# TensorE work of the last stage in column tiles of 128 rows by 32 columns

## The chip, the cores and the metric

The kernel runs on one core of one Trainium2 chip. Time is device microseconds (us) of that core; the number used is the median of the runs shown. TensorE is the matrix engine (PE in the profile, its weight loads PEld), VectorE is DVE, ScalarE is ACT, GpSimd is POOL, SyncE is SP. All DMAs of this kernel are issued by SP.

## The reference

Inputs are bfloat16, with S = 2048 rows and D = 512 columns; F is 1376. The forward pass is

```python
xn = layernorm(A_q)
k_shift = causal 4-tap filter of k with shift_k;  kv = k_shift * v
y = causal convolution of kv with ssm_k, + kv * ssm_D        # by FFT of length 2S
out = A_q + xn * y + ((xn @ w_gate) * (xn @ w_up)) @ w_down
```

What must be returned is `out` and the gradients, for a given `grad_out`, with respect to A_q, A_k, A_v, shift_k, ssm_k, ssm_D and the three weights. The kernel computes the FFTs as products with tables of sines and cosines.

## The kernel before

**Stages.** (1) Layer norm, and for six slices of F the products g, u and dh and their gradients h, dg, du, which go to DRAM (`HD`) or stay in SBUF. (2) The weight gradients (`dw_gen`). (3) The first step of the transforms (`a_gen`, through `AX`), then the middle step (`s_gen`), whose result goes to `CX` in DRAM. (4) The last stage, lines 888 to 950, from about 278 us (its first transforms still among the last weight gradients) to the end. It works in eight chunks n, each of two groups of 128 rows.

**The last stage.** For chunk n:
- `c_load(n)` (line 650) loads 1.5 MB of `CX` into one buffer `f["C"]`. There is one such buffer, so the load of chunk n+1 waits until TensorE has read chunk n.
- `last_dft(n)` (lines 694 to 702) makes the last transform step: 12 products of 64 output rows by 512 columns. Halves h = 0 and 1 go to PSUM partitions 0 to 63 and 64 to 127, so two run side by side in the array. ScalarE copies the three results out (`c_dkv`, `c_y`, `c_o5`), and VectorE multiplies and adds them.
- `c_dsk(n)` (line 739, the gradient of shift_k) sums over the rows what VectorE has multiplied, with a weight of 32 columns of ones: 8 products of 32 output rows, in four column tiles (PSUM partitions 0, 32, 64 and 96).
- `y_o(n, rr)` (line 759) is out: 11 products of 128 by 512 accumulated in one PSUM half bank of 128 by 512, read by VectorE at once, or in the last chunk by ScalarE after one more product with the identity.
- `y_x(n, rr)` (line 776) is the gradient of xn: 22 such products, then six VectorE operations and one of ScalarE, which end in the gradient of A_q.
- `dk_pair` is the gradient of k: seven VectorE operations on 128 by 1024.

The left operands of `y_o` and `y_x` (`hd_block`) are h, dg and du with F on the partitions. Those that went to DRAM are read back by a transposing DMA (`hd_load(n)`, line 616, two buffers). Those that stayed in SBUF are transposed by TensorE in `turn_gen` (line 593): batches of eight 128 by 128 transposes into one PSUM tile, copied out by ScalarE. The batches of slice NST - 1 number 12, the first with k = 0.

**What sets the order.** Every engine call goes through class `Eng` (line 143), which only records it. Consecutive TensorE calls on the same PSUM slots become one `Op`. `emit` (line 181) then emits the `Op`s in an order that is written out in `PLAN`, a packed constant, with the PSUM place of each. The scheduler of the framework is off: each engine runs its instructions in that order. Because all calls are made in `Eng.call`, nearly every line in the profile is L173.

A product with a left operand of 128 rows by c columns occupies c columns of TensorE's array. In the last stage of the kernel before, three widths alternate: 128 (`y_o`, `y_x`, transposes), 64 (`last_dft`) and 32 (`c_dsk`).

Of the kernel before, what the change touches and what calls it, by code (L numbers as in the profile page):

```python
# [18 lines left out]
D = 512  # L19
F = 1376  # L20
R = 16
NFB = 11
NST = 6
# [4 lines left out]
NCH = 8  # L28
# [9 lines left out]
def kernel(  # L38
# [24 lines left out]
    nc = tc.nc  # L63
# [17 lines left out]
    def v3(ap, a):  # L81
        return ap.rearrange("p (a b) -> p a b", a=a)

    def bfv(ap, a, b):
        return ap.bitcast(BF)[:, 0:a * b].rearrange("p (a b) -> p a b", a=a)
# [29 lines left out]
    def rF(kind="F"):  # L115
        slots.append(Slot(2, kind))
        return PV(slots[-1], lambda b: b)

    def rN(kind="G"):
        slots.append(Slot(1, kind))  # L120
        return PV(slots[-1], lambda b: b)
# [12 lines left out]
    def together():  # L134
        hold[0] = []

    def apart():
        hold[0] = None

    def fix(x):  # L140
        return x.at(x.slot.base) if isinstance(x, PV) else x

    class Eng:


        def __init__(self, name, real):
            self.name = name; self.real = real

        def __getattr__(self, meth):
            f = getattr(self.real, meth)  # L150

            def call(*a, **k):
                last = ops[-1] if ops else None
                own = []
                for x in list(a) + list(k.values()):
                    if isinstance(x, PV) and x.slot not in own:
                        own.append(x.slot)
                cols = k["rhs"].shape[-1] if meth == "matmul" and not isinstance(k["rhs"], PV) else 128
                if meth == "matmul":
                    cols = 1  # L160
                    for n in k["rhs"].shape[1:]:
                        cols *= n
                if self.name == "PE" and hold[0]:
                    o = hold[0][0]
                elif (self.name == "PE" and hold[0] is None and last is not None and last.eng == "PE" and last.slots == own
                      and last.cols + cols <= 2200 and last.prio == now[0]):
                    o = last
                else:
                    o = Op(self.name, now[0])
                    ops.append(o)  # L170
                    if self.name == "PE" and hold[0] is not None:
                        hold[0].append(o)
                o.fns.append(lambda: f(*[fix(x) for x in a], **{kk: fix(x) for kk, x in k.items()}))  # L173
                o.uses.append((meth, a, k))
                o.cols += cols
                for s in own:
                    if s not in o.slots:
                        o.slots.append(s)
            return call
# [20 lines left out]
    nc = NC  # L200
# [5 lines left out]
    MM = nc.tensor.matmul  # L206
# [4 lines left out]
    def place(shape, dt, at):  # L211
        n = 1
        for s in shape[1:]:
            n *= s
        if dt == BF:
            v = big[0:shape[0], at // 2:at // 2 + n]
        else:
            v = big[0:shape[0], at // 2:at // 2 + 2 * n].bitcast(dt)
        if len(shape) == 3:
            return v.rearrange("p (a b) -> p a b", a=shape[1])  # L220
        if len(shape) == 4:
            return v.rearrange("p (a b c) -> p a b c", a=shape[1], b=shape[2])
        return v
# [23 lines left out]
    ident = rc.tile("ident", [128, 128])  # L247
    W12 = rc.tile("W12", [128, 192])
    W1 = W12[:, 0:128]
    W2 = W12[:, 128:192]  # L250
# [22 lines left out]
    def slot(j, r):  # L273
        return RH + 1536 * ((RO[j] + r) % RING)

    def ring(j, r, n=1):
        if j != 1:
            return place([128, n, 768], BF, slot(j, r)).rearrange("p r (t f) -> p r t f", t=3)
        return place([128, n, 384], BF, slot(1, 0) + 768 * r).rearrange("p r (t f) -> p r t f", t=3)[:, :, :, 32:128]
# [146 lines left out]
    def hd_at(b, odd):  # L426
        return 640 + 128 * b if odd else 128 * ((b + 1) % 4)
# [138 lines left out]
    f = {}  # L566
# [26 lines left out]
    def turn_gen():  # L593
        for j, r0 in ((NST - 2, R - KEEP), (NST - 1, 0)):
            blk = [(r, t, b) for r in range(r0, R) for t in range(3) for b in (0, 128)]
            for k in range(0, len(blk), 8):
                pt = bfv(rN(), 8, 128)
                for i, (r, t, b) in enumerate(blk[k:k + 8]):
                    nc.tensor.transpose(pt[:, i, :], ring(j, r)[:, 0, t, b:b + 128], ident[:])
                r, b = blk[k][0], k % 6  # L600
                ACOPY(place([128, 8, 128], BF, slot(j, r) + 256 * b), pt)
                yield

    wy = {n: place([128, NFB, D], BF, 76 * KB + 11264 * i) for i, n in enumerate("dgu")}
# [8 lines left out]
    def hd_span(n):  # L613
        return (0, 1152) if 2 * n < R - KEEP else (128, 1024)
# [5 lines left out]
    def hd_block(m, t, fb):  # L620
        h = hdP[m // 2 % 2]
        a = hd_span(m // 2)[0]
        if fb == 10:
            return h[:, 3 * (m % 2) + t, 512 - a:640 - a]
        if fb >= 8 or fb >= 6 and m >= R - KEEP:
            return place([128, 6, 128], BF, slot(fb // 2 + 1, m))[:, 2 * t + fb % 2, :]
        c = hd_at(fb // 2, m % 2) - a
        return h[:, 2 * t + fb % 2, c:c + 128]
# [65 lines left out]
    def last_dft(n):  # L694
        py = f["py"] = [v3(rF(), 2) for sig in range(3)]
        C = f["C"]
        together()
        for sig in (1, 0, 2):
            for rr in range(2):
                for h in range(2):  # L700
                    MM(py[sig][64 * h:64 * h + 64, rr, :], lhsT=W2, rhs=C[:, 2 * h + rr, sig * D:sig * D + D], start=True, stop=True)
        apart()

    def c_y(n):
# [54 lines left out]
    def y_o(n, rr):  # L759
        m = f["m"][n % 2]  # L760
        end = n == NCH - 1
        for c in (slice(0, 256), slice(256, 512)) if end and rr == 1 else (slice(0, 512),):
            po = rN("y")
            for fb in range(NFB):
                MM(po[:, c], lhsT=hd_block(2 * n + rr, 0, fb), rhs=wy["d"][:, fb, c], start=(fb == 0), stop=(fb == NFB - 1 and not end))
            if end:
                MM(po[:, c], lhsT=ident[:], rhs=m[:, rr, c], start=False, stop=True)
                ACOPY(m[:, rr, c], po[:, c])
            else:
                TT(m[:, rr, c], m[:, rr, c], po[:, c], op=ALU.add)  # L770
        if end:
            st(o0[:, 2 * n + rr, :], m[:, rr, :])
        elif rr == 1:
            st(o0[:, 2 * n:2 * n + 2, :], m[:])

    def y_x(n, rr):
        r = 2 * n + rr
        rs = slice(2 * n, 2 * n + 2)
        px = rN("y")
        for t, w in ((1, "g"), (2, "u")):  # L780
            for fb in range(NFB):
                MM(px, lhsT=hd_block(2 * n + rr, t, fb), rhs=wy[w][:, fb, :], start=(t == 1 and fb == 0), stop=(t == 2 and fb == NFB - 1 and n + 1 < NCH))
        e = t = f["e"][n % 2]; dxn = f["dxn"]
        if n + 1 == NCH:
            MM(px, lhsT=ident[:], rhs=e[:, rr, :], start=False, stop=True)
            nc.scalar.activation(dxn[:, rr, :], px, ACTF.Identity, accum_out=s1[:, r:r + 1])
        else:
            STT(dxn[:, rr, :], e[:, rr, :], 1.0, px, op0=ALU.mult, op1=ALU.add, accum_out=s1[:, r:r + 1])
        STT(e[:, rr, :], dxn[:, rr, :], 1.0, xn[:, r, :], op0=ALU.mult, op1=ALU.mult, accum_out=s2[:, r:r + 1])
        r1 = slice(r, r + 1)  # L790
        TS(c2[:, r1], s2[:, r1], -1.0 / D, None, op0=ALU.mult)
        STT(c1[:, r1], s1[:, r1], -1.0 / D, rstd[:, r1], op0=ALU.mult, op1=ALU.mult)
        STT(dxn[:, rr, :], xn[:, r, :], c2[:, r1], dxn[:, rr, :], op0=ALU.mult, op1=ALU.add)
        nc.scalar.activation(t[:, rr, :], dxn[:, rr, :], ACTF.Identity, bias=c1[:, r1], scale=rstd[:, r1])
        TT(t[:, rr, :], t[:, rr, :], go[:, r, :], op=ALU.add)
        if rr == 1:
            st(o1[:, rs, :], t[:])
# [94 lines left out]
    for _ in turn_gen():  # L892
        pass
# [16 lines left out]
    for n in range(NCH):  # L910
        last = n + 1 == NCH
        t = F0 + n * DF
# [3 lines left out]
        if n >= 1 and not last:  # L916
            dk_pair(2 * n - 2)
        at(t)
        y_o(n, 0)
        if not last:  # L920
            at(t + DF * .15)
            c_y(n + 1)
        at(t + DF * .2)
        y_x(n, 0)
        if not last:
            at(O0 + OJ * (n + 1))
# [124 lines left out]
```

## Time and profile before

| | us |
|---|---|
| median of 3 runs (lowest to highest) | 432.94 (431.38 to 433.23) |
| span of the profiled execution | 429.5 |
| the median over that span | 3.4 |
| TensorE busy in the span | 419.6 |
| VectorE busy | 352.8 |
| ScalarE busy | 267.3 |
| granted TensorE clock, mean | 1.000 |

The profile holds one execution. The span runs from the first to the last instruction; launch and completion lie around it, and no time of the profiled execution as a whole is recorded, so the spread of the three runs stands for it. Times in the views are us from the span's start. In the timeline view a row is: start, duration, engine, line, operation, output <- input with the shape, xcount, and in brackets the idle time ahead of it and what ended it. "128\*64" is the part of the array that the weight occupies, rows by columns. TensorE's busy time counts overlapped matmuls and is not a measure of its peak; start-to-start times are used instead.

### The profile page before, as it was taken

What the parts mean: (1) busy time and instruction counts of PE and PEld (TensorE: products, weight loads), DVE (VectorE), ACT (ScalarE), POOL (GpSimd) and SP (SyncE); (2) the same over time, 40 slices, a digit from 0 to 9 for tenths busy, and PEclk for the clock granted to TensorE, in tenths of its full rate; (3) what the DMA queues carried; (4) which work ended last, traced back from release to release, by engine and by line L of the source; (5) the groups of instructions that cost most, each with busy time, mean ns of one, the idle gap of its engine ahead of it and who ended that gap; (6) DMA issues with size and microseconds to landing.
All of it is one profiled execution on the core that took longest, in us unless ns stands there. A gap on an engine that the chain in (4) does not pass through costs nothing.

```text
span 429.5 us, 8151 instructions
## 1 busy us (share of the span) xinstructions
PE 419.6 (98%) x3174; PEld 204.1 (48%) x3174; DVE 352.8 (82%) x684; ACT 267.3 (62%) x374; POOL 3.5 (1%) x9
## 2 busy tenths in 40 slices
PE   7999999999999999999999999889999999999996
PEld 4665455754454333544444344444444544444443
DVE  6799979998549989899999981044869989999996
ACT  2986879698554998988989963664244340313323
POOL 1000000000000000000000000000000000000000
PEclk9999999999999999999999999999999999999999
DMA  7997787959796979989989989999999999999933
GB/s 249 401 405 240 281 305 264 370 214 381 295 338 200 322 274 306 316 254 338 321 250 315 340 282 254 241 363 336 265 290 267 310 256 317 306 282 301 284 150 124
DMA packets 94878, 124.65 MB, mean 290 GB/s; under 512 B 53748, under 2 KB 63865, under 8 KB 93816
## 3 DMA queue, kind: packets, MB, share of 16 engines
q1 hardware_dynamic: 94840, 124.13, 91.7%
q8 instruction: 25, 0.41, 0.4%
q14 instruction: 13, 0.11, 0.1%
HBM read 57.10 MB, written 54.04 MB: 259 GB/s over the span
## 4 chain that ended last, share of the span: by engine, by line
PE 91%; DMA 6%; DVE 1%; SPq 1%; issue 1%; ACT 0%; ACTq 0%
PE PP L173 91%; DMA big<-CX 4%; DMA big<-in_goT_dram 1%; DVE big L173 1%; SPq L173 1%; ACT big L173 0%; ACTq L173 0%
## 5 line engine op out<-in xcount | busy, mean ns | idle before, releaser
L173 PE MATMUL PP<-big 128*128 128x512 bf16 (+9 forms) x3174 | 419.6, 347 | 5.8 <-issue 1.8
L173 PEld LDWEIGHTS <-big 128*128 128x128 bf16 (+5 forms) x3174 | 204.1, 98 | 221.0 <-issue 65.2
L173 DVE TENSOR_TENSOR big<-big 128x1024 bf16<-128x1024 bf16 (+4 forms) x465 | 269.3, 629 | 46.0 <-ACT big L173 42.6
L173 ACT CAST big<-PP 128x512 bf16<-128x512 f32 (+2 forms) x314 | 225.2, 780 | 90.0 <-PE PP L173 74.8
L173 ACT ACTIVATE big<-big 128x512 bf16<-128x512 f32 (+3 forms) x30 | 19.1, 645 | 40.8 <-DVE big L173 40.8
L173 DVE CAST big<-PP 128x512 bf16<-128x512 f32 (+1 forms) x37 | 32.3, 873 | 11.9 <-PE PP L173 10.0
L173 ACT COPY big<-PP 128x1024 bf16<-128x1024 bf16 x25 | 24.9, 1019 | 21.5 <-PE PP L173 21.5
L173 DVE SCALAR_TENSOR_TENSOR big<-big 128x1 f32<-128x1 f32 (+2 forms) x52 | 25.5, 498 | 0.6 <-ACT big L173 0.2
L173 DVE BATCH_NORM_STATS2 big<-big 128x6 f32<-128x512 bf16 x16 | 10.8, 679 | 2.7 <-DMA big<-in_x_dram 2.6
L173 DVE TENSOR_TENSOR big<-big,PP 128x512 bf16<-128x512 bf16 x14 | 9.5, 682 | 4.1 <-PE PP L173 4.0
L173 DVE SCALAR_TENSOR_TENSOR big<-big,PP 128x512 f32<-128x512 bf16 x14 | 9.5, 682 | 3.3 <-PE PP L173 3.3
L173 DVE TENSOR_SCALAR big<-big 128x1 f32<-128x1 f32 (+1 forms) x28 | 7.0, 259 | 0.2
L173 POOL MEMSET big<- 128x1536 bf16 (+2 forms) x3 | 2.8, 950 | 256.0 <-PE PP L173 252.7
L173 ACT ACTIVATE big<-PP 128x512 f32<-128x512 f32 x2 | 1.2, 598 | 5.5 <-PE PP L173 5.5
L173 DVE RECIPROCAL big<-big 128x2 f32<-128x2 f32 (+1 forms) x9 | 1.4, 155 | 3.7 <-ACT big L173 3.7
L173 DVE BATCH_NORM_AGGREGATE big<-big 128x2 f32<-128x6 f32 x16 | 2.8, 177 | 0.2
L173 ACT ACT_TABLE_LOAD x1 | 1.3, 1283 | 0.7 <-PEq L1039 0.7
L173 DVE DVE_READ_ACCUMULATOR big<-big 128x1 f32 x16 | 1.3, 81 | 0.0
L173 DVE DVE_READ_ACCUMULATOR big<-big,PP 128x1 f32 x14 | 1.1, 81 | 0.0
L173 DVE MEMSET big<- 128x1 f32 (+1 forms) x2 | 0.2, 112 | 0.8 <-PEq L1039 0.8
L173 DVE COPY big<-PP 128x1024 bf16<-128x1024 bf16 x1 | 0.7, 685 | 0.0
L173 ACT ACTIVATION_READ_ACCUMULATOR big<-PP 128x1 f32 x2 | 0.4, 194 | 0.0
(6 smaller groups left out, 0.9 us busy)
## 6 DMA issues: line engine op xcount, KB each, us to landing
HD<-big SPq DMA_DIRECT2D x32, 384.0 KB, 8.2
AX<-big SPq DMA_DIRECT2D x16, 768.0 KB, 5.1
big<-AX SPq DMA_DIRECT2D x16, 768.0 KB, 7.4
CX<-big SPq DMA_DIRECT2D x32, 384.0 KB, 4.5
out_dram<-big SPq DMA_DIRECT2D x44, 256.0 KB, 3.1
big<-CX SPq DMA_DIRECT2D x7, 1536.0 KB, 8.7
big<-in_v_dram SPq DMA_DIRECT2D x16, 256.0 KB, 6.2
big<-in_w_dram SPq DMA_DIRECT2D x4, 768.0 KB, 6.5
```

The lines of the kernel that those rows point to most:

```text
L173: o.fns.append(lambda: f(*[fix(x) for x in a], **{kk: fix(x) for kk, x in k.items()}))
```

## The change

It gives `Eng.call` an argument `part`. With `part=4`, a product with a left operand of 128 columns is recorded as four products of 32 columns each, into the four quarters of the same PSUM partitions, and a transpose as four with 32 columns of input each. The four stand one after the other in the same `Op`, each with its own weight load. `y_o`, `y_x` and all batches of transposes of the last slice but the first get `part=4`; `last_dft` is written as 24 products of 32 output rows in place of 12 of 64. `PLAN` stays, so the order of the `Op`s, the PSUM places and all DMAs stay.

```diff
+        @staticmethod
+        def parts(a, k, n):
+            if n == 1:
+                return [(a, k)]
+            w = 128 // n
+            cs = [slice(w * i, w * i + w) for i in range(n)]
+            if "lhsT" in k:
+                h = k["lhsT"].shape[1] // n
+                return [((a[0][w * i:w * i + h],) + a[1:], {**k, "lhsT": k["lhsT"][:, h * i:h * i + h]}) for i in range(n)]
+            return [((a[0][c], a[1][:, c]) + a[2:], k) for c in cs]
...
+                part = k.pop("part", 1)
...
-                o.fns.append(lambda: f(*[fix(x) for x in a], **{kk: fix(x) for kk, x in k.items()}))
-                o.uses.append((meth, a, k))
+                for aa, kw in Eng.parts(a, k, part):
+                    o.fns.append(lambda aa=aa, kw=kw: f(*[fix(x) for x in aa], **{kk: fix(x) for kk, x in kw.items()}))
+                    o.uses.append((meth, aa, kw))
...
-                    nc.tensor.transpose(pt[:, i, :], ring(j, r)[:, 0, t, b:b + 128], ident[:])
+                    nc.tensor.transpose(pt[:, i, :], ring(j, r)[:, 0, t, b:b + 128], ident[:], part=4 if j == NST - 1 and k else 1)
...
-                    MM(py[sig][64 * h:64 * h + 64, rr, :], lhsT=W2, rhs=C[:, 2 * h + rr, sig * D:sig * D + D], start=True, stop=True)
+                    for q in range(2):
+                        o = 64 * h + 32 * q
+                        MM(py[sig][o:o + 32, rr, :], lhsT=W2[:, 32 * q:32 * q + 32], rhs=C[:, 2 * h + rr, sig * D:sig * D + D], start=True, stop=True)
...
-                MM(po[:, c], lhsT=hd_block(2 * n + rr, 0, fb), rhs=wy["d"][:, fb, c], start=(fb == 0), stop=(fb == NFB - 1 and not end))
+                MM(po[:, c], lhsT=hd_block(2 * n + rr, 0, fb), rhs=wy["d"][:, fb, c], start=(fb == 0), stop=(fb == NFB - 1 and not end), part=4)
...
-                MM(po[:, c], lhsT=ident[:], rhs=m[:, rr, c], start=False, stop=True)
+                MM(po[:, c], lhsT=ident[:], rhs=m[:, rr, c], start=False, stop=True, part=4)
...
```

The product in `y_x` (line 782) and the one with the identity behind it (line 785) get `part=4` in the same way.

More of the change, by code (lines that the diff above doesn't have):

```diff
@@ L781, in y_x @@
             for fb in range(NFB):
-                MM(px, lhsT=hd_block(2 * n + rr, t, fb), rhs=wy[w][:, fb, :], start=(t == 1 and fb == 0), stop=(t == 2 and fb == NFB - 1 and n + 1 < NCH))
+                MM(px, lhsT=hd_block(2 * n + rr, t, fb), rhs=wy[w][:, fb, :], start=(t == 1 and fb == 0), stop=(t == 2 and fb == NFB - 1 and n + 1 < NCH), part=4)
         e = t = f["e"][n % 2]; dxn = f["dxn"]
         if n + 1 == NCH:
-            MM(px, lhsT=ident[:], rhs=e[:, rr, :], start=False, stop=True)
+            MM(px, lhsT=ident[:], rhs=e[:, rr, :], start=False, stop=True, part=4)
             nc.scalar.activation(dxn[:, rr, :], px, ACTF.Identity, accum_out=s1[:, r:r + 1])
```

## The prediction

> **What bounds the kernel.** I read the page's busy times, then the chain that ended last, then the waits after 290 us, where all of the change lies.
>
> ```profile
> span 429.5 us, 8151 instructions
> ...
> PE 419.6 (98%) x3174; PEld 204.1 (48%) x3174; DVE 352.8 (82%) x684; ACT 267.3 (62%) x374; POOL 3.5 (1%) x9
> ```
>
> ```profile
> 289.90 102.24 PE PP L173 x595
> 392.14 9.06 DMA big<-CX
> 401.20 0.04 issue
> 401.24 18.34 PE PP L173 x95
> ...
> 420.39 5.19 DVE big L173 x12
> ```
>
> The last 140 us are TensorE's, except for one load of C that lands as TensorE needs it, and a VectorE tail. But the chain names only what came last at each step. Busy time by stretch (TensorE, its loads, VectorE) shows a second engine with next to no slack:
>
> ```profile
> 350.00:360.00 10.00, 10.00 (x48) 4.53 (x47) 9.86 (x22) 1.82 (x3) 0.00 (x0) 1.00 1.25 233
> ...
> 390.00:400.00 10.00, 10.00 (x54) 4.74 (x52) 9.75 (x21) 3.44 (x4) 0.00 (x0) 1.00 1.06 328
> ```
>
> So what TensorE gains counts only as far as VectorE waited for it. From 340 us on, these are all the VectorE rows that show a wait (in brackets, with what ended it):
>
> ```profile
> 345.25 0.69 DVE L173 SCALAR_TENSOR_TENSOR big<-big,PP 128x512 f32<-128x512 bf16 x1 [1.80 <-PE PP L173]
> ...
> 365.66 0.69 DVE L173 TENSOR_TENSOR big<-big,PP 128x512 bf16<-128x512 bf16 x1 [0.19 <-PE PP L173]
> ...
> 376.15 0.69 DVE L173 SCALAR_TENSOR_TENSOR big<-big,PP 128x512 f32<-128x512 bf16 x1 [0.29 <-PE PP L173]
> ...
> 400.03 0.69 DVE L173 TENSOR_TENSOR big<-big,PP 128x512 bf16<-128x512 bf16 x1 [0.28 <-PE PP L173]
> ...
> 420.39 0.69 DVE L173 SCALAR_TENSOR_TENSOR big<-big 128x512 bf16<-128x512 f32 x1 [0.18 <-ACT big L173]
> ```
>
> **What goes: changes of tile width.** Whenever TensorE passes between products of 128, 64 and 32 columns, its weight loads pause for 0.42 us; these rows are TensorE's loads:
>
> ```profile
> 345.79 0.12 PEld L173 LDWEIGHTS <-big 128*32 128x32 bf16 x8 [0.42 <-issue]
> 346.33 1.00 PEld L173 LDWEIGHTS <-big 128*64 128x64 bf16 x12 [0.42 <-issue]
> 347.75 18.68 PEld L173 LDWEIGHTS <-big 128*128 128x128 bf16 x88 [0.41 <-issue]
> 366.85 1.00 PEld L173 LDWEIGHTS <-big 128*64 128x64 bf16 x12 [0.42 <-issue]
> ```
>
> The price: within the run of 88, starts lie 0.2158 us apart (18.68 less 0.11 for the first step and the last load's own length, over 86). From 345.79 to 366.85 there are 21.06 us with 2 rounds of four products of 32, 6 rounds of two of 64, and 88 full products: 96 rounds, 20.72 us. The other 0.34 us are three changes: **0.114 us each**. By the program order, the changed kernel stays at 32 columns from the second `last_dft` (289.90) on. Before, 23 changes follow: 1 at 291.3, 3 at 302, 2 at 318, 3 at 329, 3 at 346, 3 at 367, 3 at 386, 3 at 401 and 2 at 421. TensorE gains 23 x 0.114 = 2.6 us. The first `last_dft` and the products ahead of 289.90 keep their changes.
>
> **What is added: rounds of four.** From there on TensorE runs 578 rounds of four products by 512 columns, 24 by 256 and 88 by 128 (transposes), in 5520 instructions where 1536 stood. No run of many such rounds exists in the trace.
> - *512 columns.* Below: 0.2158 us, since the same 512 columns stream, and the rounds of two in `last_dft` keep 0.216 over six rounds (starts 346.573, 346.789, ...). Above: 0.226, the one step there is between the two rounds of `c_dsk` (318.389 to 318.615 counted from the last of four starts is 0.216, from the first 0.226). Full products also show 0.226 as their first step after a change and 0.216 ever after, so I take **0.2158, added cost 0**; 0.226 would add 578 x 0.0104 = 6.0 us.
> - *Transposes.* A full one takes 0.056 us (eight from 343.31 to 343.75). Below: no gain, the same 128 columns. Above: the four loads and four products of a round have to be issued in that time. After the semaphore wait that ended at 278.162, when TensorE's queue had run empty, seven instructions were issued by 278.248: 0.086 / 7 = 0.012 each, so 8 x 0.012 = 0.098 a round, +0.042 x 88 = 3.7 us. Inside a round starts lie 0.003 apart, 8 x 0.003 = 0.026, which fits. I take 0, nearest to the 0.003 row, since each batch of 64 instructions follows slow rounds in which the queue can fill.
> - *256 columns.* 24 rounds at 0.109; 8 x 0.012 fits: 0.
> - *Instruction loading.* The page has 25 packets for 6350 instructions, about 16 KB each; 3984 more instructions are 16 more packets. The packets after 290 us took 0.9 to 1.2 us for the 256 instructions that last 6.9 us in rounds of four: hidden; if not, 16 x 1 us at most.
> - SP, POOL, ACT and VectorE get no instruction more, and no wait is added.
>
> Two rules speak against the change. The Trainium skill, TensorEngine Tiling (Array Packing), Restrictions, says that column tiling switches the fast weight load off; by TensorE: Matmul & The Clock Gate, LDWEIGHTS, 128 columns would then take 107 ns, an estimate, and a transpose round would cost 51 ns more, 4.5 us in all. This trace shows loads of 94 ns for 32 columns and 98 for 128, and four of them started within 10 ns, so the row speaks for no loss. The same page (Part 1) puts the floor between matmul starts at about 25 ns, or 62 ns where microcode decodes; four at 62 are 248 ns, which would make the change a loss of tens of us. Here eight products of a round start 3 ns apart (150.620 to 150.643), but only out of a full queue.
>
> **What of it reaches the end.** TensorE's lead is 0.114 x the changes passed. VectorE can be early by no more than that, nor by more than its lead before plus the wait it had:
> - 345.25: 9 changes, 1.03; wait 1.80 is ample: 1.03.
> - 365.66: 12 changes, 1.37; 1.03 + 0.19 = 1.22.
> - 376.15: 15 changes, 1.71; 1.22 + 0.29 = 1.51.
> - 400.03: 18 changes, 2.05; 1.51 + 0.28 = 1.79.
> - 401.24, the load of C: its issue at 392.14 stands on SP behind the transposing load whose packets start at 384.59, released by TensorE when 15 changes had passed. It comes 1.71 earlier, not 2.05, so TensorE's wait of 0.39 grows to about 0.9.
> - 420.39: TensorE 1.71 + 2 changes = 1.94; VectorE 1.79 + 0.18 = 1.97: **1.94**. From there VectorE works without a break to the end.
>
> Span 429.5 - 1.9 = 427.6. The runs' median stands 3.4 us over the span, and the same edges are kept: 432.9 - 1.9 = **431.0 us**. What is late next is VectorE, with the C load beside it.
>
> **Rivals.**
> - *Rounds of four are dearer (slower).* At 0.226 us each, TensorE's 2.6 us gain becomes a loss of 6.0 - 2.6 = 3.4 us, and VectorE waits for it: 436.3. It decides from 2.6 / 578 = 0.0045 us a round; four extra ns eat the gain. For it: 0.226 is the only such step on record. Against: 64-column rounds and full products recover after the first step. Dear transposes belong here too: +3.7, nearly all before 345 us, leaves about +1.5: 434.4.
> - *Issue bound (much slower).* The densest long stretch is 83 products with their loads in 5 us (74.6 to 79.6), 0.060 us a pair. If that were the limit, a round would be 0.241: 578 x 0.025 + 24 x 0.132 + 88 x 0.185 = 34, less 2.6: about 464. Against: in that stretch nothing waits, and 0.012 each after the empty queue.
> - *The loads of C hold (no change).* DMA is busy throughout (1.06 and 1.25 above). The last three C loads landed 0.69 and 0.64 us before their use and 0.39 after. If they do not move, TensorE is not early at 401.24, and 2 changes are left: 432.7. Against: SP's issue follows TensorE.
> - *All of TensorE's gain arrives (faster)*: 2.6 us, 430.3, if VectorE's rows shorten a little.
>
> **Numbers.** Forecast (430.2 to 431.8) 0.60; C loads hold 0.12; dearer rounds or transposes 0.13; issue bound 0.07; full gain 0.08. What a measurement of this kernel tells from no change is about 0.5%, 2.2 us (below 430.8, above 435.1). The forecast lies 0.2 us inside, so it gives 0.22 to faster and 0.38 to same. Faster 0.22 + 0.08 = 0.30; same 0.38 + 0.12 and 0.02 of the dearer rounds = 0.52; slower 0.18. The range runs from the full gain, 429.8, to the dearer rounds, 436.5; it leaves out the issue bound and some spread.
>
> **What would show it.** No pause of 0.42 us in TensorE's loads after 291 us; rounds 0.216 apart for 512 columns and 0.056 for transposes; VectorE idle under 0.2 us between 345 and 420; the wait for C at 401 near 0.9. Steps of 0.22 or more, or gaps that end in "issue", would make it wrong.

## The result and the profile after

The changed kernel took 437.43 us (median of four runs, 437.22 to 438.84) against 432.69 us for the kernel before (four runs): ratio 1.0127, 95% interval 1.0092 to 1.0161. The forecast was 431.0, and its range ended at 436.5. The profiled execution took 437.61 us and spans 435.8. Medians here and below are of all runs of a kernel; ratios and their intervals leave out runs in a slower state that some executions show.

The page after, first the lines that answer to the busy times of before, then the instruction queue q8 (packets, MB, share of 16 engines) and the chain by engine and by what was waited for:

```profile
span 435.8 us, 12092 instructions
...
PE 415.1 (95%) x5123; PEld 213.5 (49%) x5166; DVE 353.2 (81%) x684; ACT 267.8 (61%) x374; POOL 3.5 (1%) x9
...
q8 instruction: 40, 0.66, 0.6%
...
PE 68%; DMA 20%; DVE 7%; issue 2%; SPq 2%; ACT 0%; DVEq 0%
PE PP L186 68%; DMA big<-HD 9%; DVE big L186 7%; DMA big<-CX 5%; DMA big<-AX 3%; SPq L186 2%; DMA big<-in_goT_dram 1%; DMA AX<-big 1%; ACT big L186 0%; DVEq L186 0%
```

The same lines before:

```profile
q8 instruction: 25, 0.41, 0.4%
...
PE PP L173 91%; DMA big<-CX 4%; DMA big<-in_goT_dram 1%; DVE big L173 1%; SPq L173 1%; ACT big L173 0%; ACTq L173 0%
```

The span is 6.3 us longer, and TensorE is not busier. (The fall of its busy time from 419.6 to 415.1 us says nothing: 4.2 us of it lie before 290 us, where 43 records of products are missing from this trace. In the last stage it is busy for 135.1 us before and 134.8 after.) So the time is not in TensorE's work. The chain says where to look. Before, TensorE held 91% of it and no load of HD stands in its line; now the transposing load of HD holds 9%, and the load of C 5% in place of 4%. The timeline of TensorE from the second `last_dft` on (start, duration, operation, in brackets the idle time ahead and what ended it) shows each place:

```profile
290.18 17.49 PE L186 MATMUL PP<-big 128*32 128x512 bf16 x369 [0.34 <-DMA big<-CX]
308.19 17.38 PE L186 MATMUL PP<-big 128*32 128x128 bf16 x384 [0.53 <-issue]
325.94 1.07 PE L186 MATMUL PP<-big 128*32 128x128 bf16 x63 [0.37 <-issue]
328.12 20.80 PE L186 MATMUL PP<-big 128*32 128x512 bf16 x444 [1.11 <-DMA big<-HD]
350.26 11.84 PE L186 MATMUL PP<-big 128*32 128x512 bf16 x216 [1.34 <-DMA big<-CX]
362.76 27.16 PE L186 MATMUL PP<-big 128*32 128x512 bf16 x500 [0.66 <-DMA big<-HD]
390.53 7.11 PE L186 MATMUL PP<-big 128*32 128x512 bf16 x152 [0.60 <-DMA big<-CX]
399.56 32.09 PE L186 MATMUL PP<-big 128*32 128x512 bf16 x632 [1.92 <-DMA big<-HD]
```

Before, the same view has two rows from 289.90 on and one wait in between, for C:

```profile
289.90 110.95 PE L173 MATMUL PP<-big 128*64 128x512 bf16 x641 [1.21 <-DMA big<-CX]
401.24 24.19 PE L173 MATMUL PP<-big 128*64 128x512 bf16 x139 [0.39 <-DMA big<-CX]
```

Now there are three waits for HD (3.7 us), two more for C (1.9 us), and pauses that end in "issue". I use one measure from here on, **TensorE's last stage**: from the first product of the second `last_dft` (289.90 before, 290.18 after) to the start of the last product. It leaves out what earlier stages differ by from run to run. Counted by starts, it grew from 135.3 to 141.2 us. The rounds alone are 578 x 0.2158 + 24 x 0.109 + 88 x 0.056 = 132.2 us. So 3.1 us of it were interruptions in the kernel before: the 23 changes of width (2.6) and the wait for C. In the changed kernel the changes are gone, and 141.2 - 132.2 = 9.0 us of new interruptions have come. The seven idle times in the rows above, from 308.19 on, make 6.5 of them; the rest are shorter pauses and restarts.

### The profile page after: what moved, and what is told of

Same layout as the page of the kernel before. It is cut to its first block, busy times and chain, and to the rows that moved or that the text cites. A ratio compares the mean times of both kernels' runs of the same rounds, so it can differ in the third digit from the quotient of the medians.

```text
span 435.8 us, 12092 instructions
## 1 busy us (share of the span) xinstructions
PE 415.1 (95%) x5123; PEld 213.5 (49%) x5166; DVE 353.2 (81%) x684; ACT 267.8 (61%) x374; POOL 3.5 (1%) x9
## 4 chain that ended last, share of the span: by engine, by line
PE 68%; DMA 20%; DVE 7%; issue 2%; SPq 2%; ACT 0%; DVEq 0%
PE PP L186 68%; DMA big<-HD 9%; DVE big L186 7%; DMA big<-CX 5%; DMA big<-AX 3%; SPq L186 2%; DMA big<-in_goT_dram 1%; DMA AX<-big 1%; ACT big L186 0%; DVEq L186 0%
## 5 line engine op out<-in xcount | busy, mean ns | idle before, releaser
L186 PE MATMUL PP<-big 128*32 128x512 bf16 (+9 forms) x5123 | 415.1, 349 | 16.5 <-issue 4.6
L186 PEld LDWEIGHTS <-big 128*32 128x32 bf16 (+4 forms) x5166 | 213.5, 97 | 217.8 <-issue 60.1
```

The costliest lines, as they stand in the source:

```text
L186: o.fns.append(lambda aa=aa, kw=kw: f(*[fix(x) for x in aa], **{kk: fix(x) for kk, x in kw.items()}))
```

## What stops the loads

The next view is the busy time in half-microseconds of the kernel *after*, around one instruction fetch: the raw records have a packet of 16 KB on the instruction queue that starts at 375.40 and takes 1.03 us. The transposing load of HD runs from 370.8 to 378.8. The last column is what all DMAs moved, in GB/s; the one before it counts a packet's whole time where it starts and so can exceed 1:

```profile
375.00:375.50 0.50, 0.50 (x16) 0.21 (x8) 0.50 (x4) 0.50 (x1) 0.00 (x0) 1.00 1.38 317
375.50:376.00 0.50, 0.50 (x16) 0.27 (x12) 0.50 (x1) 0.16 (x1) 0.00 (x0) 1.00 4.15 206
376.00:376.50 0.50, 0.50 (x16) 0.26 (x12) 0.47 (x2) 0.00 (x0) 0.00 (x0) 1.00 0.02 2
376.50:377.00 0.50, 0.50 (x16) 0.21 (x8) 0.50 (x3) 0.00 (x0) 0.00 (x0) 1.00 0.08 9
377.00:377.50 0.50, 0.50 (x16) 0.26 (x12) 0.50 (x2) 0.00 (x0) 0.00 (x0) 1.00 0.70 153
```

For over a microsecond the core's DMA moves next to nothing: half a microsecond after the fetch has begun, the whole transposing load stands still, and it goes on 0.7 to 0.8 us after the record of the fetch has ended (at 376.43 here). In the raw records its packets of 256 bytes fall from 556 in the first of these half-microseconds to 3 in the third. This happened six times in the changed kernel (stops of 1.3 to 1.5 us) and once before, because 21 fetches fell into the last stage where 6 fell before. The seven HD loads took 58.7 us in place of 51.0.

The second instruction queue (q14, packets of 8 KB, as many after as before) does the same on a smaller scale, in both kernels: in the kernel before, one of 0.34 us at 321.15 is followed by a stop of 0.65 us. So it is not only the added fetches that stop a load.

A late HD load is passed on. All DMAs are issued by SyncE in a fixed order, and a transposing load holds SyncE while it is being issued. SyncE's own rows in the changed kernel, around the largest wait, and the issue of the same load of C before:

```profile
385.07 10.94 SPq L186 DMA_TRANSPOSE big<-HD  x1
396.06 3.11 SPq L186 DMA_DIRECT2D out_dram<-big  x4
399.27 0.54 SPq L186 DMA_DIRECT2D big<-CX  x1
```

```profile
392.14 0.62 SPq L173 DMA_DIRECT2D big<-CX  x1
```

Before, this was 9.1 us ahead of its use at 401.24. So there is a loop: TensorE finishes with a buffer, HD is loaded into it, stores are issued, C is issued, TensorE needs both. Before, this loop had almost no slack (C came 0.39 us late), and the prediction saw that but did not ask what could lengthen it.

## The theories

- **A**: the added instructions bring instruction fetches; a fetch that meets a transposing load stops it, the loop has no slack, and TensorE waits. Fetches that come late themselves starve TensorE at the ends of instruction pages.
- **B**: reading the right operand four times as often from SBUF slows the DMAs.
- **C**: rounds of four are dearer than full products (the prediction's first rival).

C can be read off the trace already: rounds of four run 0.2158 us apart for 512 columns, 0.056 for transposes.

## The experiments

Medians are in us, each beside the kernel before on the same chip; 1 to 4, 5 to 8, 9 to 12 and 13 to 16 shared one.

**1. Instructions without column tiles.** The kernel before, with all products of `y_o` and `y_x` but the first of each group split in four by columns of the *right* operand:

```diff
+                for i in range(split):
+                    aa = (a[0][:, w * i:w * i + w],) + a[1:]
+                    kw = {**k, "rhs": k["rhs"][:, w * i:w * i + w], "stop": k["stop"] and i == split - 1}
```

> The kernel before, in which each product of y_o and y_x except the first of a group is written as four products of a quarter of its columns (128 output rows each, the same weight loaded four times). TensorE gets 3036 instructions more (3984 in the change), the right operand is still read once, the widths still change. By the step rows (0.0558 us for 128 columns against 0.2158 / 4) TensorE alone needs 484 x 0.0074 = 3.6 us more. Theory A (instruction fetches): the 12 more packets of 16 KB stop transposing loads for about 1.4 us each where they fall into them, as in the changed kernel, and TensorE pauses at some boundaries of 256 instructions; transposing loads 8 to 9 us on the mean against 7.3 before, TensorE waits for them; 438 to 442 us. Theory B (fourfold reading of the right operand slows the DMAs): no hole beyond the one or two of before, loads 7.3 us, about 436. Theory C (what costs is the rounds of four themselves): also about 436.

Measured: 438.80 (before 432.78), ratio 1.0100, 1.0017 to 1.0184. TensorE's last stage is 142.1 us, 6.8 over before; of these, 506 split products at 4 x 0.0558 - 0.2158 = 0.0074 us each explain 3.7. There are four full stops of HD loads at fetches (at 302.55, 341.7, 358.65 and 373.5), the seven loads took 58.6 us, and TensorE waits for HD (2.5 us) and C (0.5 us). So more instructions alone, each right operand read once, lengthen the loads as much as the change does: against B. The waits are about half of those of the changed kernel (3.0 against 5.6 us); that a TensorE which is itself 3.7 us slower needs its buffers later would fit, but was not tested.

**2 and 3. No transposing load.** Both kernels with ordinary loads of HD in place of the transposing ones:

```diff
-        ldT(out=hdP[n % 2][:, :, 0:b - a], in_=HP[n, a:b])
+        ld(hdP[n % 2][:, :, 0:b - a], HP[n, a:b].rearrange("(p x) e -> p (x e)", p=128).rearrange("p (k w) -> p k w", k=6))
```

For the kernel before:

> The kernel before with the eight transposing loads replaced by ordinary loads of the same bytes, row after row, so the left operands of y_o and y_x that come from DRAM are in the wrong places. It is the base for the next run. All theories: the loads are shorter, the wait of 0.39 us for C goes; 431.5 to 432.7 us.

For the changed kernel:

> The changed kernel with the same ordinary loads (operands in the wrong places as in the run before). Theory A: with no transposing load to stop and none for the fetches to queue behind, the gain comes out: 1.5 to 2.6 us less than the run before it, and no pause at 256-instruction boundaries. Theory B: the reading of four streams still slows ordinary loads; no gain or a loss against the run before it, 0 to 3 us more. Theory C: a loss of some us.

Measured: 428.76 (ratio to before 0.9916, 0.9883 to 0.9950) and 427.91 (0.9889, 0.9835 to 0.9943). The loss is gone; whether a gain is left, these runs do not tell: the medians differ by 0.9 us, where A expected 1.5 to 2.6. Runs 13 and 14 below repeat the pair. A's other sign failed: TensorE still pauses at ends of instruction pages without transposing loads, for 0.9 us in this trace:

```profile
337.34 82.69 PE L186 MATMUL PP<-big 128*32 128x512 bf16 x1623 [0.91 <-issue]
```

The kernel without transposing loads was faster than I expected by 3 us.

**4. `last_dft` alone in tiles of 32.** 192 more instructions and, by the program order, no width of 64 left:

> Only last_dft in 24 products of 32 rows; the rest as before. Six changes between 32 and 64 go, 192 instructions are added (three quarters of one packet). Theory A: 6 x 0.114 = 0.7 us less on TensorE, 0.3 to 0.7 of it at the end, 432.0 to 432.4; one packet may fall otherwise, plus or minus 1. Theories B and C: the few rounds weigh little, the same.

Measured: 433.14, ratio 1.0003, 0.9974 to 1.0033: no difference that can be measured, in either direction. The small gain that A expected is not confirmed.

**5 and 6. Loads of HD in two halves.** If late HD is the cause, then loading first the rows that the first group needs should take TensorE's waits for HD away:

```diff
+        ldT(two=[dict(out=hdA[n % 2][:, :, 0:640 - a], in_=HP[n, a:640]), dict(out=hdB[n % 2][:, :, 0:b - 640], in_=HP[n, 640:b])])
```

On the changed kernel:

> The changed kernel with each transposing load of HD issued as two, one behind the other: first the rows that the first group of 128 needs (and the piece that both groups share), then the rest. Nothing else is moved, the same bytes travel, TensorE's instructions are those of the changed kernel. TensorE now waits for the first half at the first group and for the second at the second group. Theory A (the loss comes by late transposing loads, which instruction fetches stop, and by late loads of C behind them): the three waits of TensorE for HD, 1.1, 0.8 and 1.9 us, go, as the first half lands some 4 us earlier; waits for C (2.3 us) and pauses at the ends of instruction pages (1.3 us) stay: 437.4 - 3.8 = 433 to 434.5. If the time is lost elsewhere (TensorE's own rounds, VectorE): no change, 437 to 438.

On the kernel before:

> The kernel before with the same split loads. It has no wait for HD, and 0.46 us for C. Theory A: 432 to 433.5, no difference that can be measured. If splitting helps by itself (say by an earlier queue), it is below 431.

Measured: 443.80 (1.0271, 1.0209 to 1.0334) and 435.38 (1.0080, 1.0045 to 1.0116; above the 432 to 433.5 expected. In its trace the last stage took 135.7 us, so nearly all of this lies in earlier stages). The expectation of 433 to 434.5 for the changed kernel was plainly wrong. These two rows of TensorE in the changed kernel with split loads are typical:

```profile
351.97 39.04 PE L187 MATMUL PP<-big 128*32 128x512 bf16 x716 [2.27 <-DMA big<-CX]
394.25 16.78 PE L187 MATMUL PP<-big 128*32 128x512 bf16 x300 [3.25 <-DMA big<-CX]
```

TensorE's waits for HD fell from 3.7 to 0.9 us as expected, but those for C rose from 2.3 to 6.2. The wait moved along the loop; it did not go. Seven fetches fell into these loads, and they took 63.0 us in all. One fetch stopped everything for 1.45 us; at the six others the rate fell to between 20 and 200 GB/s for over a microsecond, and to about 10 GB/s at the end. Why the halves take longer than the whole is not settled.

**7 and 8. Long packets without instructions.** The kernel before, and ScalarE issues 20 copies in the last stage, of one packet of 16 KB each, or of 256 bytes each as a control:

```diff
+                if ops[i].eng == "ACT" and na > NACT - 60 and na % 3 == 0:
+                    real.scalar.dma_start(SCR[q:q + 1, :], big[4 * q:4 * q + 1, 38912:47104])
```

With 16 KB:

> The kernel before, and in the last stage ScalarE also issues 20 copies of one 16 KB packet each (from one SBUF partition to an unused place in DRAM), behind every third of its operations. TensorE's instructions and the output are those of the kernel before. The packets are the size of instruction fetches, with no instruction added. Theory A, in the form that any 16 KB packet stops a transposing load: about 8 of the 20 meet a transposing load, each stops it for about 1.3 us, and the time is 3 to 6 us over that of the same kernel with packets of 256 bytes: 436 to 439. If only instruction fetches do it, or the stops and the fetches merely coincide: the same as with small packets, 432.5 to 434.

With 256 bytes:

> The same 20 copies with 256 bytes each in place of 16 KB: the same instructions, waits and queues on ScalarE and SyncE, without the long packets. It is the control for the run before it. All theories: 432.5 to 434, what the added issues and their waits on shared semaphores cost; the transposing loads show no stops beyond those at instruction fetches.

Measured: 438.05 and 435.56 (before 433.18): long against short, by the runs' means, 1.0060, about 1.001 to 1.011. (The control itself is 2.4 us over the kernel before, above its expectation of 432.5 to 434; its last stage shows 1.0 of it.) The effect is 2.5 us, a little under the 3 to 6 expected, and the trace says why. The kernel with long packets, in half-microseconds; a packet starts at 341.05 while HD is being transposed:

```profile
341.00:341.50 0.50, 0.50 (x7) 0.32 (x5) 0.47 (x3) 0.00 (x0) 0.00 (x0) 1.00 1.53 307
341.50:342.00 0.50, 0.50 (x9) 0.38 (x7) 0.50 (x2) 0.00 (x0) 0.00 (x0) 1.00 0.96 88
342.00:342.50 0.50, 0.50 (x6) 0.26 (x5) 0.50 (x2) 0.00 (x0) 0.00 (x0) 1.00 1.27 290
```

Eight packets met a running load, as expected (a ninth came together with a fetch), but these packets take 0.61 to 0.66 us where fetches take 0.9 to 1.2, and the stops last 0.2 to 0.55 us in place of 1.4. So a long packet that is no instruction fetch also stops a transposing load, for a shorter time. TensorE's waits for HD (2.1 us) and C (2.3 us) appear in the kernel before with no instruction added to TensorE; the control shows one wait of each, 1.2 and 2.0 us.

**9 and 10. C ahead of the stores.** The last four loads of C are moved up in SyncE's order, right behind the transposing load:

```diff
+            for i in [i for i in order if getattr(ops[i], "C", 0) >= 4]:
+                at_ = order.index(i)
...
+                order.insert(max(to, rd) + 1, order.pop(at_))
```

On the changed kernel:

> The changed kernel with the last four loads of C moved forward in SyncE's order: each is issued right behind the transposing load of HD that it stood behind, ahead of the one to six stores and small loads that were issued between them. TensorE's instructions are those of the changed kernel. By the loop theory (TensorE frees a buffer, the transposing load runs for 7 to 10 us and holds SyncE, then stores are issued, then C, which TensorE needs for the next chunk; the stops at instruction fetches lengthen this loop, which had no slack) C comes 0.5 to 3.9 us earlier, TensorE's waits for C (2.3 us) go and part of the waits for HD behind them: 433 to 435. If the DMA engines are simply full, so that the order does not matter, or if the stores, now later, make VectorE wait: 437 or more.

On the kernel before:

> The kernel before with the same move of the last four loads of C. It has one wait for C of 0.46 us to lose: 432 to 433, no difference that can be measured. A loss would show that the stores' delay costs VectorE more than the loads gain.

Measured: 445.49 (1.0285, 1.0225 to 1.0346) and 438.20 (1.0135, 1.0077 to 1.0194): worse in both. In the changed kernel C's waits went (2.3 to 1.0 us), but the stores behind it now held VectorE, which wants their buffers. VectorE in the kernel before with C moved:

```profile
365.99 1.90 DVE L173 TENSOR_TENSOR big<-big 128x1024 bf16<-128x1024 bf16 x3 [3.97 <-DMA out_dram<-big]
...
384.34 0.69 DVE L173 TENSOR_TENSOR big<-big 128x1024 bf16<-128x1024 bf16 x1 [1.92 <-DMA out_dram<-big]
```

So the expected 433 to 435 was wrong, and the other outcome on record, stores that make VectorE wait, came true. This move did not win back the microseconds that the transposing loads lose; other orders were not tried.

**11. Half the depth.** Tiles of 64 columns (`part=2`, `last_dft` as before):

> The change at half its depth: full products and transposes of the last stage in two tiles of 64 columns, last_dft as before in tiles of 64, so that two of three width changes a chunk stay and one goes. 1264 more instructions than before, against 3984 of the changed kernel: five more instruction fetches, not sixteen. Theory A (the loss follows the number of fetches that meet a transposing load): a third of the loss, 433.5 to 435.5. If it is the number of column tiles or the repeated reading of the right operand, by tiles per round: half of the loss or more, 435 to 437; if any split of the products costs the same: 437.

Measured: 434.29, ratio 1.0055, 1.0019 to 1.0091: 1.65 us over the kernel before where the changed kernel on this chip (12) is 5.05 over it, a third of the loss, as A has it. The interval, 0.8 to 3.9 us, does not exclude the half that tiles per round would give. Its trace has 11 fetches in the last stage and three stops.

**12. The changed kernel again:**

> The changed kernel once more, on the chip of the other runs of this call: 436 to 439, and in its trace again six or seven stops of a transposing load at instruction fetches, pauses of TensorE at program rows that are 256 apart, and no pause at a change of width after 292 us. If stops and pauses lie at other rows by chance, the rows of the pauses should still be the same modulo 256.

Measured: 437.69, ratio 1.0114, 1.0049 to 1.0179. Five stops where six or seven were expected, at fetches that start at 305.75, 322.47, 375.69, 398.09 and 414.06, each within 1.5 us of one in the first trace; last stage 141.3 us. One short pause at the end of a page, where the first trace had four.

**13 to 16. Long packets and instructions where nothing is transposed.** Four kernels with the ordinary loads of experiments 2 and 3. The base:

> The kernel before with ordinary loads of HD (same bytes, not transposed, so the left operands stand in wrong places), on the chip of the other runs of this call: 428 to 430. It is the base for the three others.

The changed kernel:

> The changed kernel with the same ordinary loads of HD. Theory A: without transposing loads to stop, the 2.2 us of TensorE's width changes are left as a gain, less pauses of 0.3 to 1.4 us at the ends of instruction pages: 0.8 to 1.9 us below the base. If the loss comes from the instructions or from reading the right operand four times, whatever the loads are: 3 to 6 us above the base.

The base with 16 KB copies:

> The base with the 20 copies of one 16 KB packet each from ScalarE. Theory A (only a transposing load is stopped as a whole by one long packet): within 1 us of the same kernel with packets of 256 bytes. If long packets slow any load as much: 2.5 us above it, as with the transposing loads.

The base with 256-byte copies:

> The base with the 20 copies of 256 bytes each: the control for the run before it. 428 to 432: what the added issues and their waits cost.

Measured: 429.47, 427.65, 429.84, 429.75. (One of the twelve runs with 16 KB copies took 1515 us, for a reason that no trace shows; the median of the other eleven is 429.45.) The change against its base: -1.8 us by the medians, -1.2 by the means, ratio of the means 0.9972, 0.9938 to 1.0006: in A's direction but not clear of no change, and far from the +3 to +6 of B. Long against short packets: between -0.3 us (eleven runs) and +0.1 (all), where it was +2.5 with transposing loads. One caution: an ordinary load holds SyncE for 0.4 to 1.3 us (13 and 14), a transposing one for 7.7 to 13.2 (before and after the change), so these kernels have more slack as well. But at fetches and copies in the middle of an ordinary load the traces of 14 and 15 show no stop. TensorE's last stage in the changed kernel without transposing loads has only these two interruptions in this view:

```profile
315.22 66.73 PE L186 MATMUL PP<-big 128*32 128x512 bf16 x1351 [0.39 <-issue]
382.56 38.65 PE L186 MATMUL PP<-big 128*32 128x512 bf16 x784 [0.61 <-DMA big<-CX]
```

**All traces beside each other** (one trace each, from the raw records; fetches of 16 KB in the last stage; a stop is over 1.15 us at a fetch, within a transposing load, in which all DMAs together move under 25 GB/s):

```
kernel                          instr. added  fetches  stops         seven HD loads  last stage
before                                     0        6      1            51.0 us        135.3 us
halves, before (6)                         0        6      1            53.0           135.7
small copies (8)                           0        6      1            51.1           136.3
last_dft in 32 (4)                       192        6      2            56.0           137.6
tiles of 64 (11)                        1264       11      3            55.3           137.9
16 KB copies (7)                           0        6      1, 8 short   54.8           139.6
the change                              3984       21      6            58.7           141.2
the change again (12)                   3984       21      5            57.5           141.3
split by columns (1)                    3036       17      4            58.6           142.1 (3.7 TensorE's own)
halves, changed (5)                     3984       21      1, 6 part    63.0           145.9
no transposing load (13)                   0        -      -               -           134.8
the change, no transposing load (14)    3984        -      -               -           134.1
```

Counted from 1.0 us on, the kernel before, (1), (4) and (8) have one stop more each, at the edge of a load. The last stage follows the length of the HD loads, within some 3 us. The loads are also slowed by what they overlap with at their start, so stops alone do not order the rows (experiment 4, which has two stops, long loads, and no difference in its runs' median). Experiments 9 and 10 are left out: there VectorE was the cause.

## Why the prediction was wrong, point by point

- **The step that failed** is "Instruction loading": "hidden; if not, 16 x 1 us at most". The number of packets was right (25 to 40 on the page, 15 more), but the price was asked only of TensorE, whether 256 instructions last longer than their fetch. The cost lies on another engine: on the load that a fetch meets. 15 more fetches in the last stage brought five more stops of 1.3 to 1.5 us, 7.7 us more of HD loads in all, and TensorE's last stage grew by 5.9. Removing the transposing loads takes the loss away (3, 14); adding packets without instructions brings part of it (7); adding them where nothing is transposed brings none (15 against 16); a third of the instructions brings about a third (11).
- The step also stated an upper bound of 16 us and then gave it no rival, no chance and no place in the range. The range ended at 436.5 by another rival's price; the bound would have told me that it was the largest unknown.
- **"Hidden" was not quite right for TensorE either.** The pauses that end in "issue" lie at these rows of TensorE's program order:

```
changed kernel             5295  5551  6319  7087
the same again (12)        9647
no transposing load (3)    5295  6063  7087
no transposing load (14)   5295  6063
```

  All are 175 modulo 256: the ends of pages of 256 instructions. In the first trace TensorE is idle there for 0.1 to 0.5 us each, 1.3 us in all; in experiment 3 for up to 0.9. At each of these rows TensorE goes on 2.3 to 3.2 us after the start of the fetch ahead of it, which fits fetches that came too late for it. The Trainium skill, Runtime: NRT & Kernel Launch, Instruction fetch mechanics, has instructions fetched in blocks of 16 KiB, 256 instructions, ahead of their use, and calls the cost of a boundary mostly hidden. The block size agrees (40 packets, 0.66 MB). "Mostly hidden" holds for most of the boundaries here, but not for these, and it says nothing of what a block does to other transfers; the runs decide.
- **What goes** was right: 23 changes at 0.114 us, 2.6 us. Without transposing loads the kernel before shows 134.8 - 132.2 = 2.6 us of interruptions in its last stage, all at changes of width (13).
- **What is added** was right but for the instruction loading: 0.2158 us for 512 columns, sustained, and 0.056 for transposes in most batches of eight (some took 0.04 us longer in all, one 0.2). The count of what stood before is a slip without effect: 780 products from 289.90 on are 1560 instructions, not 1536. Both rules that spoke against it stayed without effect, and so did the rivals "rounds of four are dearer" and "issue bound".
- **What of it reaches the end** fell with the step above. VectorE's waits were summed as if TensorE were always early. With nothing transposed, -1.9 us lies within what was measured (-1.8 by medians, -1.2 by means, interval -2.7 to +0.3 us), but no change does too, and in the traces of 13 and 14 the last stage is only 0.7 us shorter. So this part is neither refuted nor confirmed.
- **The rival "the loads of C hold"** had the right place and the wrong mechanism: C is late, because HD ahead of it on SyncE is late.
- **What would show it**: the pauses of 0.42 us at changes of width after 291 us are gone (one of 0.43 at 300.89 is the end of a page) and the rounds are right; VectorE's waits and the wait for C are not. "Gaps that end in 'issue' would make it wrong" was the one warning that came true, and it is the smaller part.

## What to carry to other kernels

A change that multiplies instructions also adds DMA packets, 16 KB for every 256 instructions; before calling them hidden, look at which transfers run while they are fetched, and above all at transposing loads. Where a chain of loads on one queue has no slack in the profile (a C load that lands 0.4 us late, DMA share near 1), price everything that can lengthen one of them, not only what the edit moves. A bound that is written down has to go into the range, or be excluded by a row.

## What was not expected of the hardware

- One long packet stops a transposing load as a whole: for 1.2 to 1.5 us at a fetch of 16 KB (0.9 to 1.2 us), 0.6 to 0.7 us at most fetches of 8 KB (0.3 to 0.4 us), 0.2 to 0.55 us at a copy of 16 KB from one partition (0.61 to 0.66 us). Why a fetch costs more than such a copy is open. Ordinary loads show no such stop in their middle and no loss (429.84 against 429.75).
- TensorE's clock can drop after a wait. In experiment 12 TensorE waited 3.47 us for HD up to 330.35; the windows of that trace, with the granted clock third from the end:

```profile
326.80:330.20 3.40, 0.08 (x8) 0.00 (x0) 3.07 (x7) 2.62 (x3) 0.00 (x0) 1.00 1.16 353
330.30:333.30 3.00, 2.95 (x36) 1.25 (x40) 1.40 (x4) 0.00 (x0) 0.00 (x0) 0.66 0.89 273
333.30:336.00 2.70, 2.70 (x44) 1.22 (x40) 1.35 (x2) 0.22 (x1) 0.00 (x0) 0.75 1.26 256
336.00:340.00 4.00, 4.00 (x80) 1.95 (x76) 3.18 (x6) 2.42 (x3) 0.00 (x0) 1.00 1.07 218
```

  Eight rounds then lie 0.41 us apart in place of 0.216: a wait of 3.5 us costs 1.5 us more than itself. The same followed idle times of 3.25 us in experiment 5 (granted clock 0.50 from 394.3 to 397.7), 2.34 us in experiment 9 (0.50 from 351.8 to 355.2) and 2.03 us in experiment 10 (0.50 from 371.7 to 375.0), but not one of 2.39 us in experiment 9 (1.00 from 393.9 to 398.0). Each time the slow stretch lasted 3.4 us in the raw records. The Trainium skill, TensorE: Matmul & The Clock Gate, Part 1, gives an idle window of about 3.4 us that runs freely. The length of the slow stretch agrees with it; the waits do not, since 2.03 and 2.34 us were enough, and what decides between these and the 2.39 is open.
- The rounds of four column tiles of 32 cost TensorE no more than one full product: four loads and four products in each 0.2158 us, 37 instructions per microsecond, in a stretch of 66.7 us without a break in this view in experiment 14.
